# Linformer attention and an MLP mixer on one core: gated loads of batch 3, E and F cast by DMA, and the sums of two batches on one engine

## The chip, the core and the metric

The kernel runs on one core of one Trainium2 chip. The metric is the time in microseconds (us) that the device takes for one execution; lower is better. A second number, the span, is the time from the first to the last instruction of the one execution that was profiled; the profiled execution's own time is a little longer than its span.

## The reference

The inputs are q, k and v, each [8 batches, 8 heads, 1024 positions, 64], two projections E and F of shape [64, 1024], and four mixer weights, all float32. Cut to what is computed:

```python
k_proj = einsum('ks,bhsd->bhkd', E, k)             # 1024 positions -> 64
v_proj = einsum('ks,bhsd->bhkd', F, v)
scores = (q @ k_proj.T) / sqrt(64)
attn = exp(scores - max) / sum(exp(scores - max))
x = heads_side_by_side(attn @ v_proj)              # [8, 1024, 512]
h = relu(x.T @ w_tok1) @ w_tok2                    # mixes tokens, 1024 -> 256 -> 1024
u = x + h.T
out = u + relu(u @ w_ch1) @ w_ch2                  # mixes channels, 512 -> 1536 -> 512
```

## The kernel before

Batches are software-pipelined on one core. While TensorE works on the channel mixing of batch b (the "up" product with w_ch1, then the "down" product with w_ch2), the projections, attention and token mixing of the next batches are put between its steps. The order is written out by hand: every step of up and down has a cost in us (0.43, 0.66 and so on), the costs add up to a clock, and a list of items (time on that clock, function) says before which step an item is issued (lines 688 to 725). Each engine then executes its instructions strictly in the order in which they were issued.

**What a batch goes through.** load (line 85) reads q, k and v of a batch by DMA, issued on GpSimd (POOL), which also casts float32 to bfloat16; each of the three buffers exists once, so a load waits until the batch before has been read out of it. kv_step (line 228) projects k and v with E and F: 16 matmuls, in turn one that reads k and one that reads v (lines 157 and 162); after them it issues the three loads of the batch after. turn_q (line 99) transposes q by two DMAs on SyncE's queue (SP). score_step (189) and ou_step (202 to 214) are the attention of one head; the VectorE (DVE) instruction in line 209 writes x. tok1_steps (247) and tok2_steps (270) mix the tokens; line 273 adds x and so makes u. After every second slab of u a DMA transpose on SP (line 275) writes a quarter of uT, the left factor of the up product. SP holds these transposes, those of q and the output stores (line 599) in one order.

**Up and down.** Both are Strassen-Winograd products with seven partial products P1 to P7 (lines 518 and 576), apart from the up product of batch 0, which is plain (line 444). Winograd needs sums of quarter matrices: up_t (lines 496 to 502) makes T1, T2, T4 and a difference in place from uT; up_weights (472 to 478) makes those of w_ch1, down_weights (659) those of w_ch2, once each; up_sum (427 to 433) makes S1, S2, S4 and a difference in place from g, the activation between up and down. Up runs in three rounds of two slabs (i = 0, 2, 4); for every pair of slabs four sums fall due, one at each of the next four calls of up_sum. In line 425 `third` says who computes them: 0 POOL, 1 DVE for the first two and POOL for the last two, 2 DVE. In batch 0 a sum is 128x512 and there are six groups of four; from batch 1 on a sum is 128x1024 and there are three groups of four. relu_add (line 524) is DVE's step in up: it adds a saved partial product K to one in PSUM and clips at zero. In down, snap (line 482) saves a partial product on ScalarE (ACT) and POOL adds u to it (611, 625, 631).

**The front.** Before any of this the first batch is loaded in four pairs of heads. E and F come first, by two DMAs on SP in float32 into EF_f; ACT casts one half (line 146), DVE the other (147); TensorE transposes the result (150), and DVE copies it to EFT (151). Then come q's transposes on TensorE (315) and the first kv_step in pieces.

**The place that the change is named for.** kv_step(2) is issued at clock 34.4 of batch 0, and its loads of batch 3 were issued right behind it. At about the same clock tok2_steps(1) ends (30.0 to 34.2) and issues the last quarters of uT of batch 1. up_t(1) is issued at 37.1 and needs all four quarters; batch 1's up product cannot go past P2 before it. kv_step(3), the first user of batch 3's k and v, is issued 13.8 into batch 1.

Of the kernel before, what the change touches and what calls it, by code (L numbers as in the profile page):

```python
# [10 lines left out]
F32 = mybir.dt.float32  # L11
# [6 lines left out]
def kernel(  # L18
# [13 lines left out]
    nc = tc.nc  # L32
# [59 lines left out]
        )  # L92

    def load_all(b):
        load(b, "k", k)
        load(b, "v", v)
        load(b, "q", q)

    def turn_q(b):
        st["qT", b] = work.tile([P, H, 4, P], BF16, tag="qT", name="qT", bufs=1)  # L100
# [5 lines left out]
            )  # L106


    EF_f = work.tile([P, S], F32, tag="o1", name="EF_f", bufs=2)
    EF_sb = work.tile([P, S], BF16, tag="T1", name="EF_sb", bufs=1)  # L110
    nc.sync.dma_start(out=EF_f[0:KP], in_=E)
    nc.sync.dma_start(out=EF_f[KP:P], in_=F)
    wc1_v = moe_w_ch1.rearrange("(dc p) c -> p dc c", p=P)
    wc2_v = moe_w_ch2.rearrange("(cc p) d -> p cc d", p=P)

# [30 lines left out]
    nc.scalar.activation(out=EF_sb[:, 0:512], in_=EF_f[:, 0:512], func=ACT.Copy)  # L146
    nc.vector.tensor_copy(out=EF_sb[:, 512:S], in_=EF_f[:, 512:S])
    e_ps = b_ps("e_ps", BF16)
    for si in range(SC):
        nc.tensor.transpose(e_ps[:, si * P : (si + 1) * P], EF_sb[:, si::SC], ident)  # L150
    nc.vector.tensor_copy(out=EFT.rearrange("p s k -> p (s k)"), in_=e_ps)


    def k_mm(b, kv_ps, hs, si, f):
# [73 lines left out]
    def kv_step(b):  # L228
        st["kp", b] = work.tile([KP, H, 2, D], BF16, tag="kprojs", name="kprojs", bufs=1)
        st["kv", b] = kv_ps = front_ps("kv_ps")  # L230
        for si in range(SC):
            f = dict(start=(si == 0), stop=(si == SC - 1))
            k_mm(b, kv_ps, AL, si, f)
            v_mm(b, kv_ps, AL, si, f)
        k_out(b, kv_ps, AL)
        if b + 1 < B:
            load(b + 1, "q", q)
            load(b + 1, "k", k)
            load(b + 1, "v", v)

    def tok1_steps(b):
        def step(t, s0):
# [174 lines left out]
    def up_sum(b):  # L417

        if not st["sq", b]:
            return  # L420
        i, n, m = st["sq", b].pop(0)
        a11, a12, a21, a22 = (g_part(b, i, n, r, c) for c in range(2) for r in range(2))
        s1, s2, s4 = (x[:, i : i + n, :] for x in st["S", b])
        third = (i + n - 1) // 2
        eng = (nc.gpsimd, nc.gpsimd if m > 1 else nc.vector, nc.vector)[third]
        if m == 0:
            eng.tensor_add(out=s1, in0=a21, in1=a22)  # L427
        elif m == 1:
            eng.tensor_sub(out=s2, in0=s1, in1=a11)  # L429
        elif m == 2:  # L430
            eng.tensor_sub(out=a21, in0=a11, in1=a21)  # L431
        else:
            eng.tensor_sub(out=s4, in0=a12, in1=s2)  # L433
# [16 lines left out]
    def up_plain(b, part=()):  # L450

        g = st["g", b]
        for n in range(24):
            i, r = divmod(n, 4)
            cc, sh = (i, CH + i)[r // 2], r % 2
            up_mm(b, n, [DMC - 1] if n in part else range(DMC))
            o = g[:, cc, sh * 512 : (sh + 1) * 512]
            nc.scalar.activation(out=o, in_=st["g_ps", n], func=ACT.Relu)
            up_sum(b)
            if r == 3:  # L460
                up_sums(b, i, 1)
            if n in (6, 10, 14):
                up_weights((n - 6) // 4)
            yield 0.22 if n in part else 0.87
        up_weights(3)

    def up_weights(n):

# [94 lines left out]
    def down(b):  # L563
# [23 lines left out]
        def v2(t):  # L587
            return t.rearrange("p (e d) -> p e d", e=2)
# [12 lines left out]
        def part(j, m):  # L601
# [19 lines left out]
            elif m == 5:  # L621
                x["ga"] = c_ps("ga")
                yield from prod(x["ga"], "P5", j, True)
                x["K5"] = snap("K5", x["ga"])
                nc.gpsimd.tensor_add(out=v2(x["K5"]), in0=v2(x["K5"]), in1=u[:, bot, hi])  # L625
                if first:
                    down_weights(2)
            elif m == 6:
                yield from prod(x["be"], "P6", j)
                x["K2"] = snap("K2", x["be"])  # L630
                nc.gpsimd.tensor_add(out=v2(x["K2"]), in0=v2(x["K2"]), in1=u[:, top, hi])
                if first:
                    down_weights(3)
            elif m == 3:
                yield from prod(x["ga"], "P3", j, stop=True)
                nc.vector.tensor_add(out=x["o1"][:, :, hi], in0=v2(x["ga"]), in1=v2(x["K2"]))
                store(j, "o1", top)
            elif m == 7:
                yield from prod(x["be"], "P7", j)
                nc.vector.tensor_add(out=x["o2"][:, :, hi], in0=v2(x["be"]), in1=v2(x["K5"]))  # L640
                store(j, "o2", bot)
            else:
                yield from prod(x["be"], "P4", j, stop=True)
                nc.vector.tensor_add(out=x["o2"][:, :, lo], in0=v2(x["be"]), in1=u[:, bot, lo])
                store(j, "o2", bot)
# [43 lines left out]
    for b in range(B):  # L689
        up_us = 18.28 if b == 0 else 18.06  # L690
        dn = t0 + up_us
        if b == 0:
# [3 lines left out]
            add(t0 + 30.0, 0.6, tok2_steps(1))  # L696
            add(t0 + 37.1, 0.43, [lambda n=n: up_t(1, n) for n in range(4)])
            kv(t0 + 34.4, 2, 2.4)
            items.append((t0 + 29.6, lambda: turn_q(2)))
        else:  # L700
            if b == 1:
                attend(t0 + 1.0, 2, 1.3)
                add(t0 + 14.6, 0.45, tok1_steps(2))
                add(dn + 0.5, 0.8, tok2_steps(2))
# [51 lines left out]
```

## Time and profile before

| | us |
|---|---|
| median of 3 runs | 464.19 (463.48 to 465.42) |
| the profiled execution | 466.96 |
| its span | 465.2 |
| busy in the span: TensorE (PE) | 418.4 |
| VectorE (DVE) | 300.0 |
| GpSimd (POOL) | 224.4 |
| ScalarE (ACT) | 201.3 |

Times of instructions are counted from the start of the span. A row of the timeline gives the start, how long a run of like instructions took, the engine, the line in the kernel, out<-in, the shapes and how many there were; in square brackets stands how long the engine sat idle before it and what released it. A row of the windows gives, for one stretch, each engine's busy time and instruction count, then the clock granted to TensorE as a share of full speed, the DMA engines' busy share, and GB/s. A DMA row ends with the median time from issue to landing.

### The profile page before, as it was taken

To read this page: it belongs to the slowest core of one execution; us is meant where nothing else is said; L and a number is where in the kernel's file an instruction comes from. 1 tells how busy PE (TensorE), PEld (TensorE's weight loads), DVE (VectorE), ACT (ScalarE), POOL (GpSimd) and SP (SyncE) were. 2 spreads that over 40 slices of the span, in tenths; PEclk is the share of its full clock that TensorE was granted. 3 is DMA by queue.
4 is the path that set the end of the run, shared out by engine and by line. 5 is a ranking of instruction groups with operands and counts; after the bars stand their busy time and mean duration, and the time that the engine had idled before them with its cause. 6 is when DMAs were issued, how large, how long until landed. Compare 5 with 4: busy or idle time off the path is not lost.

```text
span 465.2 us, 7577 instructions
## 1 busy us (share of the span) xinstructions
PE 418.4 (90%) x2985; PEld 270.4 (58%) x3012; DVE 300.0 (64%) x500; ACT 201.3 (43%) x368; POOL 224.4 (48%) x161
## 2 busy tenths in 40 slices
PE   2779987991799999999999999999999999999896
PEld 2466445660344774478545874488447854685385
DVE  1545579360786767585867586767768686845842
ACT  2636662211465136533464345623762355316321
POOL 7431944230084262934394366637373439354841
PEclk9989998997699999999999999999999999999899
DMA  8999989699746968399529934994703420242013
GB/s 161 207 204 205 180 118 202 149 153 195 175 90 107 195 153 182 54 187 214 153 40 196 212 126 91 145 212 114 166 1 58 125 90 2 47 136 92 0 46 135
DMA packets 92691, 61.83 MB, mean 133 GB/s; under 512 B 59888, under 2 KB 88048, under 8 KB 92656
## 3 DMA queue, kind: packets, MB, share of 16 engines
q0 software_dynamic: 29200, 29.36, 39.5%
q1 hardware_dynamic: 63456, 31.99, 30.3%
q8 instruction: 23, 0.38, 0.3%
q14 instruction: 12, 0.10, 0.1%
HBM read 59.24 MB, written 16.78 MB: 163 GB/s over the span
## 4 chain that ended last, share of the span: by engine, by line
PE 72%; DVE 14%; DMA 7%; ACT 3%; issue 2%; SPq 0%; DVEq 0%; ACTq 0%
PE be L518 14%; PE be L576 14%; PE ga L518 7%; PE ga L576 6%; DMA uT<-u_sb 6%; PE h_ps L247 5%; PE al L576 4%; PE al L518 4%; PE g_ps L444 4%; PE u_ps L270 4%; DVE g L524 3%; PE ou_ps L202 3%; PE kv_ps L157 3%; DVE u_sb L273 2%; DVE x_sb L209 2%
## 5 line engine op out<-in xcount | busy, mean ns | idle before, releaser
L482 ACT ACTIVATE K<-be 128x512 f32<-128x512 f32 x116 | 67.1, 600 | 83.6 <-PE be L518 37.2
L576 PEld LDWEIGHTS <-g 128*128 128x128 bf16 x768 | 74.8, 98 | 17.5 <-issue 0.4
L576 PEld LDWEIGHTS <-S 128*128 128x128 bf16 x576 | 56.0, 98 | 12.0 <-issue 0.3
L194 ACT ACTIVATE attnT<-sco 128x512 bf16<-128x512 f32 x64 | 37.7, 595 | 53.0 <-PE sco L189 51.4
L427 POOL TENSOR_TENSOR S<-g 128x1024 bf16<-128x1024 bf16 (+1 forms) x9 | 17.2, 1907 | 85.3 <-DVE g L524 70.3
L611 POOL TENSOR_TENSOR K<-K,u_sb 128x512 f32<-128x512 f32 x16 | 19.2, 1198 | 69.2 <-ACT K L482 69.2
L518 PEld LDWEIGHTS <-wc 128*128 128x128 bf16 x336 | 32.1, 99 | 34.5 <-issue 1.5
L518 PEld LDWEIGHTS <-uS 128*128 128x128 bf16 x252 | 24.9, 100 | 44.7 <-issue 18.6
L576 PE MATMUL be<-wc,g 128*128 128x256 bf16 x384 | 49.3, 273 | 0.2
L273 DVE TENSOR_TENSOR u_sb<-u_ps,x_sb 128x512 bf16<-128x512 f32 x56 | 38.4, 687 | 12.3 <-PE u_ps L270 11.5
L518 PE MATMUL be<-uT,wc 128*128 128x512 bf16 x168 | 46.3, 385 | 0.0
L482 ACT ACTIVATE K<-ga 128x512 f32<-128x512 f32 x58 | 33.5, 608 | 29.3 <-PE ga L576 24.4
L209 DVE TENSOR_TENSOR x_sb<-ou_ps,rdn 128x512 bf16<-128x512 f32 x64 | 44.3, 692 | 2.2
L524 DVE CUSTOM_DVE_ANT_0 g<-be,K 128x512 bf16<-128x512 f32 x42 | 27.6, 686 | 23.4 <-PE be L518 22.7
L431 POOL TENSOR_TENSOR g<-g 128x1024 bf16<-128x1024 bf16 (+1 forms) x18 | 37.1, 2062 | 3.6 <-DVE S L427 3.6
L625 POOL TENSOR_TENSOR K<-K,u_sb 128x512 f32<-128x512 f32 x16 | 19.4, 1214 | 38.2 <-ACT K L482 38.2
L518 PE MATMUL be<-T,uS 128*128 128x512 bf16 x84 | 24.4, 391 | 13.2 <-DVE T L498 13.2
L433 POOL TENSOR_TENSOR S<-g,S 128x1024 bf16<-128x1024 bf16 (+1 forms) x18 | 35.4, 1967 | 0.7 <-DVE S L429 0.7
L202 PE MATMUL ou_ps<-vbd,attnT 128*128 128x130 bf16 x256 | 25.8, 225 | 10.8 <-DVE x_sb L209 8.3
L559 ACT ACTIVATE g<-be 128x512 bf16<-128x512 f32 x42 | 23.5, 596 | 25.3 <-PE be L518 25.3
L524 DVE CUSTOM_DVE_ANT_0 g<-al,K 128x512 bf16<-128x512 f32 x42 | 27.6, 686 | 7.5 <-PE al L518 4.4
L270 PE MATMUL u_ps<-R_sb,wt 128*128 128x512 bf16 x98 | 30.3, 379 | 2.3 <-DVE u_sb L273 1.9
(92 smaller groups left out, 766.9 us busy)
## 6 DMA issues: line engine op xcount, KB each, us to landing
out_dram<-o SPq DMA_DIRECT2D x32, 512.0 KB, 2.9
q_sb<-in_q_dram POOLq DMA_DIRECT2D x7, 1024.0 KB, 9.5
k_sb<-in_k_dram POOLq DMA_DIRECT2D x7, 1024.0 KB, 14.0
v_sb<-in_v_dram POOLq DMA_DIRECT2D x7, 1024.0 KB, 20.4
wc<-in_moe_w_ch_dram POOLq DMA_DIRECT2D x4, 384.0 KB, 14.8
wc<-in_moe_w_ch_dram POOLq DMA_DIRECT2D x2, 768.0 KB, 32.5
q_sb<-in_q_dram POOLq DMA_DIRECT2D x4, 256.0 KB, 7.7
k_sb<-in_k_dram POOLq DMA_DIRECT2D x4, 256.0 KB, 8.2
```

The costliest lines, as they stand in the source:

```text
L194: nc.scalar.activation(out=at, in_=sco, func=ACT.Exp, scale=scale)
L202: nc.tensor.matmul(ou[:, s // 2, o : o + 2 * D1], at[:, s * P : (s + 1) * P], vbd[:, h, :], start=True, stop=True,)
L209: nc.vector.tensor_tensor(out=st["x", b][:, :, h * D : (h + 1) * D].rearrange("p (b k) d -> p b k d", b=2), in0=ov[:, :, :, 0:D], in1=rdn[ ...
L270: nc.tensor.matmul(u_ps, wt2[:, t, s::SC], st["R", b][:, t, :], start=(t == 0), stop=(t == TC - 1))
L273: nc.vector.tensor_add(out=st["u", b][:, s, :], in0=u_ps, in1=st["x", b][:, s, :])
L431: eng.tensor_sub(out=a21, in0=a11, in1=a21)
L433: eng.tensor_sub(out=s4, in0=a12, in1=s2)
L482: nc.scalar.activation(out=t, in_=x, func=ACT.Copy)
L518: nc.tensor.matmul(acc, l[:, dc, i * P : (i + 1) * P], r[:, :, dc, :], start=start and dc == 0, stop=stop and dc == 1, skip_group_check=True,)
L524: nc.vector._custom_dve(TENSOR_ADD_SAT, out=o, in0=x, in1=y, s0=3.0e38, s1=0.0)
L559: nc.scalar.activation(out=g_part(b, i + e, 1, 1, 0)[:, 0], in_=be[e], func=ACT.Relu)
L576: nc.tensor.matmul(acc[:, e * HF : (e + 1) * HF], l[:, lc + c, l0 + (2 * j + e) * P : l0 + (2 * j + e + 1) * P], r[:, rc + c, r0 : r0 + HF ...
```

## The change

It has six edits. (1) kv_step(2) no longer issues the loads of batch 3. A new gated_load(3), an item at clock 1.5 of batch 1, first copies one column of uT of batch 1, from the slabs that the last quarter's transpose writes, on POOL, and then issues the three loads; they stand behind that copy in POOL's order. (2) E and F are loaded on POOL, cast by the DMA, ahead of the first loads of q, k and v; EF_f and its two casts go, and the copy to EFT is split between DVE and ACT. (3) `third` is 2 in the first and the last batch, so DVE makes all sums there. (4) up_weights(3) moves from the end of up of batch 0 to the end of part (j=1, P7) of down of batch 0, between DVE's eviction and the store. (5) turn_q(2) is issued at 25.2 instead of 29.6, which puts it ahead of one output store on SP. (6) load_all now issues q, k, v, the order that kv_step used.

```diff
+    nc.gpsimd.dma_start(out=EF_sb[0:KP], in_=E)
+    nc.gpsimd.dma_start(out=EF_sb[KP:P], in_=F)
-    nc.sync.dma_start(out=EF_f[0:KP], in_=E)
-    nc.sync.dma_start(out=EF_f[KP:P], in_=F)
...
-    nc.scalar.activation(out=EF_sb[:, 0:512], in_=EF_f[:, 0:512], func=ACT.Copy)
-    nc.vector.tensor_copy(out=EF_sb[:, 512:S], in_=EF_f[:, 512:S])
...
-    nc.vector.tensor_copy(out=EFT.rearrange("p s k -> p (s k)"), in_=e_ps)
+    nc.vector.tensor_copy(out=eft[:, 0:512], in_=e_ps[:, 0:512])
+    nc.scalar.activation(out=eft[:, 512:], in_=e_ps[:, 512:], func=ACT.Copy)
...
-        if b + 1 < B:
-            load(b + 1, "q", q)
-            load(b + 1, "k", k)
-            load(b + 1, "v", v)
+        if b + 1 < B and b != 2:
+            load_all(b + 1)
+
+    def gated_load(b, x):
+
+        gate = work.tile([P, 1], BF16, tag="gate", name="gate", bufs=1)
+        nc.gpsimd.tensor_copy(out=gate, in_=x)
+        load_all(b)
...
-        third = (i + n - 1) // 2
+        third = 2 if b in (0, B - 1) else (i + n - 1) // 2
...
-        up_weights(3)
...
                 nc.vector.tensor_add(out=x["o2"][:, :, hi], in0=v2(x["be"]), in1=v2(x["K5"]))
+                if (b, j) == (0, 1):
+                    up_weights(3)
                 store(j, "o2", bot)
...
-            items.append((t0 + 29.6, lambda: turn_q(2)))
+            items.append((t0 + 25.2, lambda: turn_q(2)))
...
+                items.append((t0 + 1.5, lambda: gated_load(3, st["uT", 1][:, SC - 1, DMC - 1, 0:1])))
```

Three places show what this does to the order of instructions. Lines of the changed kernel are two to four higher than those of before for the same code (up_sum is 430 to 436, relu_add 526, down_weights 663, the POOL adds 613 to 633).

POOL where batch 0 goes over into batch 1. K_... are the saved partial products of down of batch 0, S_... and g belong to up of batch 1. Before:

```order
L625 TENSOR_TENSOR K_1053<-K_1053,u_sb 128x512
L631 TENSOR_TENSOR K_1082<-K_1082,u_sb 128x512
L90 DMA q_sb<-in_q_dram 128x8x512
L90 DMA k_sb<-in_k_dram 128x8x512
L90 DMA v_sb<-in_v_dram 128x8x512
L427 TENSOR_TENSOR S_1194<-g 128x1024
```

The changed kernel in the same place:

```order
L627 TENSOR_TENSOR K_1053<-K_1053,u_sb 128x512
L633 TENSOR_TENSOR K_1079<-K_1079,u_sb 128x512
L241 COPY gate<-uT 128x1
L90 DMA q_sb<-in_q_dram 128x8x512
L90 DMA k_sb<-in_k_dram 128x8x512
L90 DMA v_sb<-in_v_dram 128x8x512
L430 TENSOR_TENSOR S_1186<-g 128x1024
```

The loads keep their place among POOL's instructions, but the gate now stands ahead of them, and behind it stand the sums of batch 1.

DVE where up of batch 0 goes over into down of batch 0. x_sb<-ou_ps is the attention of batch 1, wc_68 is w_ch1, dT_72 the first difference of w_ch2. Before:

```order
L433 TENSOR_TENSOR S_136<-g,S_135 128x512
L208 RECIPROCAL rdn<-ou_ps 128x8
L209 TENSOR_TENSOR x_sb<-ou_ps,rdn 128x8x64
L478 TENSOR_TENSOR wc_68<-wc_68 128x2x768
L427 TENSOR_TENSOR S_134<-g 128x512
L659 TENSOR_TENSOR dT_72<-wc_69 128x1536
L208 RECIPROCAL rdn<-ou_ps 128x8
L209 TENSOR_TENSOR x_sb<-ou_ps,rdn 128x8x64
```

The changed kernel:

```order
L436 TENSOR_TENSOR S_134<-g,S_133 128x512
L207 RECIPROCAL rdn<-ou_ps 128x8
L208 TENSOR_TENSOR x_sb<-ou_ps,rdn 128x8x64
L430 TENSOR_TENSOR S_132<-g 128x512
L663 TENSOR_TENSOR dT_72<-wc_69 128x1536
L207 RECIPROCAL rdn<-ou_ps 128x8
L208 TENSOR_TENSOR x_sb<-ou_ps,rdn 128x8x64
```

up_weights(3), the row with wc_68, has left this place; it now stands between the second and the last pair of u_sb of batch 1.

DVE in up of batch 7, rounds i = 2 and the start of i = 4. g<-al, g<-be and g<-ga are relu_add. Before:

```order
L524 ISA g<-ga,K_4719 128x512
L524 ISA g<-al,K_4752 128x512
L524 ISA g<-al,K_4758 128x512
L524 ISA g<-be,K_4782 128x512
L524 ISA g<-be,K_4787 128x512
L524 ISA g<-ga,K_4773 128x512
L524 ISA g<-ga,K_4777 128x512
L427 TENSOR_TENSOR S_4692<-g 128x1024
L429 TENSOR_TENSOR S_4693<-S_4692,g 128x1024
```

The changed kernel:

```order
L526 ISA g<-ga,K_4719 128x512
L430 TENSOR_TENSOR S_4692<-g 128x1024
L432 TENSOR_TENSOR S_4693<-S_4692,g 128x1024
L526 ISA g<-al,K_4752 128x512
L434 TENSOR_TENSOR g<-g 128x2x512
L526 ISA g<-al,K_4758 128x512
L436 TENSOR_TENSOR S_4694<-g,S_4693 128x1024
L526 ISA g<-be,K_4782 128x512
L526 ISA g<-be,K_4787 128x512
```

Four sums that POOL made beside DVE now stand in DVE's own order, two ahead of the two relu_adds of P2 and two between and behind them; the next round gets two more than it had.

More of the change, by code (lines that the diff above doesn't have):

```diff
@@ L94, in load_all @@
     def load_all(b):
+        load(b, "q", q)
         load(b, "k", k)
         load(b, "v", v)
-        load(b, "q", q)
     def turn_q(b):
@@ L106, in turn_q @@
             )
-    EF_f = work.tile([P, S], F32, tag="o1", name="EF_f", bufs=2)
     EF_sb = work.tile([P, S], BF16, tag="T1", name="EF_sb", bufs=1)
-    nc.sync.dma_start(out=EF_f[0:KP], in_=E)
-    nc.sync.dma_start(out=EF_f[KP:P], in_=F)
+    nc.gpsimd.dma_start(out=EF_sb[0:KP], in_=E)
+    nc.gpsimd.dma_start(out=EF_sb[KP:P], in_=F)
     wc1_v = moe_w_ch1.rearrange("(dc p) c -> p dc c", p=P)
@@ L150 @@
         nc.tensor.transpose(e_ps[:, si * P : (si + 1) * P], EF_sb[:, si::SC], ident)
-    nc.vector.tensor_copy(out=EFT.rearrange("p s k -> p (s k)"), in_=e_ps)
+    eft = EFT.rearrange("p s k -> p (s k)")
+    nc.vector.tensor_copy(out=eft[:, 0:512], in_=e_ps[:, 0:512])
+    nc.scalar.activation(out=eft[:, 512:], in_=e_ps[:, 512:], func=ACT.Copy)
     def k_mm(b, kv_ps, hs, si, f):
```

## The prediction

> **What bounds the kernel now.** I read the page first, then the table of waits, then windows around each place where TensorE (PE) stands still. The page gives PE nearly the whole span:
>
> ```profile
> PE 418.4 (90%) x2985; PEld 270.4 (58%) x3012; DVE 300.0 (64%) x500; ACT 201.3 (43%) x368; POOL 224.4 (48%) x161
> ```
>
> So a gain can only be PE's idle time, or time at a lower clock. The waits name the largest: PE's P6 of batch 1 waits for DVE, and DVE for a transpose.
>
> ```profile
> DVE T L496 <- DMA uT<-u_sb: 14.7, 2, 12.6
> ...
> PE be L518 <- DVE T L498: 13.2, 1, 13.2
> ```
>
> The windows show three stalls (PE's busy time is the second number), and behind each one a stretch at clock 0.50; the row from 119.30 to 138.70 covers batch 1's up as far as kv_step(3).
>
> ```profile
> 68.10:72.20 4.10, 0.03 (x1) 0.00 (x0) 4.07 (x6) 0.05 (x1) 4.10 (x3) 0.99 1.14 178
> 72.20:75.50 3.30, 3.28 (x17) 2.32 (x18) 2.59 (x5) 0.60 (x1) 0.13 (x1) 0.50 1.22 201
> 105.80:119.30 13.50, 0.33 (x3) 0.05 (x2) 1.41 (x3) 0.53 (x1) 0.00 (x0) 0.64 1.21 218
> 119.30:123.30 4.00, 4.00 (x13) 1.71 (x13) 2.82 (x6) 2.28 (x4) 0.00 (x0) 0.50 1.20 251
> 119.30:138.70 19.40, 18.39 (x99) 8.39 (x98) 16.68 (x32) 12.54 (x23) 9.94 (x5) 0.90 0.53 103
> ...
> 437.30:440.70 3.40, 3.40 (x10) 1.17 (x8) 1.18 (x3) 1.19 (x2) 3.04 (x2) 0.50 0.00 0
> ```
>
> In the chain of waits the last quarter of uT of batch 1 takes 17.80 us from issue to its user, those of batches 2 and 3 take 4.77 and 3.89:
>
> ```profile
> 99.90 17.80 DMA uT<-u_sb
> ...
> 164.17 4.77 DMA uT<-u_sb
> ...
> 214.47 3.89 DMA uT<-u_sb
> ```
>
> What differs is what runs beside it. The timeline has the three loads of batch 3 issued from 98.12 on, and the DMA engines are full until 119.30 (share 1.21):
>
> ```profile
> 98.12 0.92 POOL L90 DMA_DIRECT2D q_sb<-in_q_dram  x1 [3.82 <-DMA qT<-q_sb]
> ...
> 101.26 0.87 POOL L90 DMA_DIRECT2D k_sb<-in_k_dram  x1 [2.21 <-PE kv_ps L162]
> ...
> 102.35 0.89 POOL L90 DMA_DIRECT2D v_sb<-in_v_dram  x1 [0.22 <-issue]
> ...
> 117.83 0.69 DVE L496 TENSOR_TENSOR T<-uT 128x1024 bf16<-128x1024 bf16 x1 [12.57 <-DMA uT<-u_sb]
> ...
> 119.30 1.87 PE L518 MATMUL be<-T,uS 128*128 128x512 bf16 x4 [13.17 <-DVE T L498]
> ...
> 138.69 0.40 PE L157 MATMUL kv_ps<-k_sb,EFT 128*64 128x512 bf16 x1
> ```
>
> **The gate.** Without the loads the last quarter should need 4.3 us, between 3.89 and 4.77. It starts later, though: up_weights(3) now stands on DVE ahead of the last two evictions of u, and costs what a 128x1536 difference costs alone, 0.95 us (row below), some of it in a gap; I charge 0.8. uT is there at 99.9 + 0.8 + 4.3 = 105.0. P6 follows 119.30 - 117.83 = 1.5 later, at 106.6, 12.7 us earlier than before. Without that idle time the 4.00 us at clock 0.50 go as well: 2.0 us. So PE would be ready for kv_step(3) at 138.69 - 14.7 = 124.0. DVE had 16.68 us of work in these 19.40 us and hardly lets PE come sooner.
>
> What is late next is batch 3's v: kv_step(3) reads k and v in turn. Behind the gate POOL issues q at about 105.3 (the copy of one column is bounded by nothing and by 0.9, a DMA issue), k at 106.2 and v at 107.1. Behind those stand only POOL's sums of batch 1, not due until well after. v's landing time after issue was 22.4 us in the loads of batch 3, 18.3 in those of batch 2 and 19.9 in those of batch 4:
>
> ```profile
> v_sb<-in_v_dram POOLq DMA_DIRECT2D x1, 1024.0 KB, 22.4
> ...
> v_sb<-in_v_dram POOLq DMA_DIRECT2D x1, 1024.0 KB, 18.3
> ...
> v_sb<-in_v_dram POOLq DMA_DIRECT2D x1, 1024.0 KB, 19.9
> ```
>
> I take 19, since the transposes that slowed the first are done and those of q of batch 3 come only near the end. v is there at 126.1, 2.1 us after PE is ready: the gain is 138.69 - 126.1 = **12.6 us**. The ends: landing after 22.4, with one more stretch at clock 0.50 (3.40 us, half of it lost: 1.7), leaves 138.69 - 129.5 - 1.7 = 7.5; PE held by nothing but DVE gives 14.3.
>
> By the Trainium skill ("TensorE: Matmul & The Clock Gate", Part 1: The HAM clock gate) the half rate comes after at least one idle window of about 3.4 us; by that a wait of 2.1 us would cost no clock. This trace differs: the 2.06 us wait at 436.93 (below) was followed by 3.40 us at 0.50. By the row the sum would be 1.7 us smaller, by the page as it stands.
>
> turn_q(2) moves past one store on SP: q's transposes go out earlier, in part beside batch 2's loads, and only the first score of batch 2, well into batch 1, needs them. I cost this at nothing; if the cover were gone, the gate would wait for the SP queue and the term above would shrink towards its lower end.
>
> **Sums of batch 0 on DVE.** Beside POOL's sums DVE's own took up to 1.37 us, alone 0.42. Twelve more at 0.42 are 5.0 us, spread over up of batch 0, where PE waits for nothing on DVE. What counts is the turn from up to down:
>
> ```profile
> 55.30 1.37 DVE L427 TENSOR_TENSOR S<-g 128x512 bf16<-128x512 bf16 x1
> ...
> 62.58 0.42 DVE L431 TENSOR_TENSOR g<-g 128x512 bf16<-128x512 bf16 x1
> ...
> 66.28 1.93 DVE L478 TENSOR_TENSOR wc<-wc 128x1536 bf16<-128x1536 bf16 x1
> ...
> 69.42 1.90 DVE L659 TENSOR_TENSOR dT<-wc 128x1536 bf16<-128x1536 bf16 x1
> ...
> 71.24 0.20 DVE L208 RECIPROCAL rdn<-ou_ps 128x8 f32<-128x8 f32 x1
> ...
> 72.22 0.61 PE L202 MATMUL ou_ps<-vbd,attnT 128*128 128x130 bf16 x4 [4.09 <-DVE x_sb L209]
> ...
> 74.83 0.95 DVE L659 TENSOR_TENSOR dT<-wc,dT 128x1536 bf16<-128x1536 bf16 x1
> ```
>
> Three DVE steps delay the reciprocal at 71.24. L478 leaves; the sum and L659 remain. At the prices alone they end at 66.3 + 0.4 + 0.95 = 67.7, a gain of 3.5; at the slowed ones at 66.3 + 1.4 + 1.9 = 69.6, a gain of 1.6. No sum runs on POOL any more, so I take the first, **3.4 us**. The 3.30 us at clock 0.50 give little beyond, as DVE is the limit behind them; half of what they cost goes into the upper end, 4.1.
>
> **Sums of batch 7 on DVE.**
>
> ```profile
> 425.84 1.08 ACT L559 ACTIVATE g<-be 128x512 bf16<-128x512 f32 x2 [1.39 <-PE be L518]
> 426.07 1.03 PE L518 MATMUL be<-uT,wc 128*128 128x512 bf16 x4
> ...
> 428.66 1.03 PE L518 MATMUL ga<-T,uS 128*128 128x512 bf16 x4
> ...
> 432.12 1.03 PE L518 MATMUL be<-uT,wc 128*128 128x512 bf16 x4
> ...
> 433.78 2.50 DVE L429 TENSOR_TENSOR S<-S,g 128x1024 bf16<-128x1024 bf16 x1
> ...
> 436.93 1.61 PE L518 MATMUL ga<-T,uS 128*128 128x512 bf16 x4 [2.06 <-DVE g L524]
> ...
> 442.11 1.47 PE L576 MATMUL be<-wc,g 128*128 128x256 bf16 x12
> ...
> 443.06 0.69 DVE L429 TENSOR_TENSOR S<-S,g 128x1024 bf16<-128x1024 bf16 x1
> ```
>
> Round i = 2 takes 432.12 - 426.07 = 6.05 us, round i = 4 takes 9.99: a sum slowed to 2.50 holds up P2's relu_adds, P5 finds no free bank for 2.06 us, and the clock falls. That loss of 3.9 goes, but now three sums stand ahead of the second relu_add of P2 in both rounds. They start when ACT has written g, 0.85 into the round, and that relu_add ends 0.85 + 3 x 0.69 + 2 x 0.65 = 4.2 in (0.65 from the pairs' spacing, an estimate); P5's second half wants the bank at 428.66 + 0.43 - 426.07 = 3.0. PE waits 1.2 in each round, 2.5 in all. The gain is 3.9 - 2.5 = **1.4 us**; ends -0.5 (a clock drop again) and 3.8.
>
> **E and F.**
>
> ```profile
> 4.07 0.72 POOL L90 DMA_DIRECT2D q_sb<-in_q_dram  x1
> ...
> 8.87 0.43 PE L150 MATMUL e_ps<-ident,EF_sb 128*128 128x128 bf16 x2 [8.87 <-ACT EF_sb L146]
> ...
> 12.69 0.61 PE L315 MATMUL qt_ps<-ident,q_sb 128*128 128x128 bf16 x4
> ```
>
> PE starts at 8.87 behind the cast. It can start up to 2 us sooner, but needs the second pair of heads next, which PE used at 12.69 and which landed near 11 (6.8 us after 4.07):
>
> ```profile
> q_sb<-in_q_dram POOLq DMA_DIRECT2D x1, 256.0 KB, 6.8
> ```
>
> Two more issues at 0.72 stand ahead of every load. So the gain lies between -0.5 and 1.2; I take **0.5 us**.
>
> **Sum.** 12.6 + 3.4 + 1.4 + 0.5 = 17.9 us. The profiled execution took 466.96 (span 465.2), so 449.1; it stands 2.8 above the median of the runs, 464.19, and carried over to that the forecast is **446.3 us**. The ends of all terms are 8.1 and 23.4, or 440.8 to 456.1.
>
> **Rivals.** *The wait moves to kv_step(3).* The loads now start late, beside two output stores, and q's transposes of batch 3 cross the last of them. If v lands 24 us after issue, at 131, and the clock drops (1.7), the gate's term is 6.0 and the time 452.9. For it: 22.4 with transposes beside. Against: those were four quarters in the middle of the loads. Chance 0.20.
>
> *The change does not free uT.* If the transposes were slow for another reason than the loads, or the gate let the loads go too early, 12.6 would vanish: 458.9. The 4.77 and 3.89 speak against it. Chance 0.07.
>
> *DVE becomes the bound in batches 0 and 7: slower.* If the moved sums kept their slowed prices, twelve at 1.37 and six at 2.50 are 31.4 us of DVE. If half of that lies on the path (an estimate; the page has DVE busy for 64%), 15.7 us are lost and the 3.4 and 1.4 with them, against 13.1 kept: 2.6 us slower, 466.8. It decides where more than 13.1 of the 31.4 us lie on the path. For it: DVE fills the stall at 68.10 (4.07 of 4.10). Against: the prices alone, 0.42 and 0.69, make 9.2 us, less than the 13.1 if all of it lay there, and POOL has no sums in these batches. Chance 0.07.
>
> **How the numbers follow.** The forecast has 0.66. 441.5 to 455 holds nearly all of it and the first rival; outside lie the other two and the tails, about 0.2. A measurement of this kernel can tell about 0.5%, 2.3 us, from no change: faster 0.92 (forecast, first rival, most of the second), same 0.03, slower 0.05.
>
> **What would show it.** The wait of T (L496 before) for uT under 1 us; no clock of 0.50 between the start of batch 1 and kv_step(3); PE's kv_step(3) idle 1 to 4 us on v_sb; the reciprocal wait at the start of down of batch 0 about 1 us; two waits near 1.2 us in batch 7 and no sum on DVE above 1 us there. I am wrong if uT still takes over 8 us, if PE stands at kv_step(3) for over 6, or if DVE's sums stay above 1 us.

## The result and the profile after

| | before | changed |
|---|---|---|
| median of 4 runs, us | 464.81 (463.48 to 465.75) | 453.01 (452.44 to 454.44) |
| the profiled execution, us | 466.96 | 452.44 |
| its span, us | 465.2 | 450.7 |

The ratio is 0.9753, 95% interval 0.9716 to 0.9789. Of the runs below, one execution of before (2442.84 us) and one of turn_late (462.22 us, at a granted clock of 0.938 on average) lie far outside the others and are left out. The time lies in the range of the forecast and 6.7 us above its value: by the profiled executions 14.5 us were gained where the sum said 17.9, by the medians 11.8. The page of the changed kernel gives PE a larger share of a shorter span; POOL lost 28 us of work. DVE took it over and is 1.2 us below before all the same: beside POOL's sums a 128x512 sum had taken it up to 1.37 us and a 128x1536 difference 1.9, and now they take about 0.42 and 0.95; the cast of half of E and F and half of the copy to EFT, 0.7 us together, are gone too.

```profile
PE 417.6 (93%) x2985; PEld 270.4 (60%) x3012; DVE 298.8 (66%) x517; ACT 201.1 (45%) x368; POOL 196.3 (44%) x146
```

In the table of waits of the changed kernel (total, times, longest) P6's wait of 13.2 us for DVE's T has shrunk to 0.6. DVE's wait of 12.6 us for uT is gone; a wait for uT of 9.3 us stands on POOL's gate instead, where PE does not feel it. Behind the first instruction's wait at the start of the kernel, PE's longest are now x_sb in the turn from up to down of batch 0 and v in kv_step(3).

```profile
POOL gate L241 <- DMA uT<-u_sb: 9.3, 1, 9.3
...
PE ou_ps L201 <- DVE x_sb L208: 7.0, 7, 3.4
...
PE kv_ps L161 <- DMA v_sb<-in_v_dram: 2.4, 2, 2.1
...
PE be L520 <- DVE T L500: 0.6, 1, 0.6
```

The windows show the same. Before, PE was busy for 14.87 of the 29 us from 96 to 125:

```profile
96.00:125.00 29.00, 14.87 (x92) 8.00 (x93) 11.66 (x20) 7.05 (x12) 2.68 (x3) 0.76 1.10 187
```

In the changed kernel it is busy for 24.15 of them, at clock 1.00. The stall of batch 0's turn is still there (first row), and behind it and behind the wait for v there is a stretch at half clock. The last two rows belong to a point that comes below: the share of the DMA engines is 1.07 in the first 160 us and 0.53 in the rest.

```profile
69.00:72.44 3.44, 0.00 (x1) 0.01 (x1) 3.41 (x6) 0.60 (x1) 1.54 (x1) 1.00 1.20 192
...
73.50:76.90 3.40, 2.97 (x17) 2.07 (x16) 2.69 (x5) 1.19 (x2) 0.15 (x1) 0.51 1.24 208
96.00:125.00 29.00, 24.15 (x153) 11.91 (x154) 24.39 (x43) 16.40 (x30) 15.15 (x10) 1.00 1.02 177
124.50:128.00 3.50, 3.50 (x16) 1.52 (x16) 0.00 (x0) 0.18 (x1) 0.87 (x1) 0.54 0.96 206
0.00:160.00 160.00, 135.59 (x1043) 87.54 (x1052) 96.60 (x182) 71.68 (x131) 56.89 (x61) 0.98 1.07 180
160.00:450.70 290.70, 281.97 (x1944) 182.85 (x1961) 202.25 (x335) 129.46 (x237) 139.42 (x86) 1.00 0.53 113
```

The timeline of the changed kernel answers the rows that were shown of before:

```profile
64.84 0.88 POOL L90 DMA_DIRECT2D q_sb<-in_q_dram  x1 [34.79 <-DMA qT<-q_sb]
65.71 0.88 POOL L90 DMA_DIRECT2D k_sb<-in_k_dram  x1
66.58 0.89 POOL L90 DMA_DIRECT2D v_sb<-in_v_dram  x1
67.47 1.19 POOL L613 TENSOR_TENSOR K<-K,u_sb 128x512 f32<-128x512 f32 x1
68.69 0.69 DVE L619 TENSOR_TENSOR o<-al,K 128x512 f32<-128x512 f32 x1 [1.34 <-POOL K L613]
...
70.16 1.38 DVE L434 TENSOR_TENSOR g<-g 128x512 bf16<-128x512 bf16 x1
...
72.44 0.40 PE L201 MATMUL ou_ps<-vbd,attnT 128*128 128x130 bf16 x4 [3.44 <-DVE x_sb L208]
...
94.96 0.95 DVE L480 TENSOR_TENSOR wc<-wc 128x1536 bf16<-128x1536 bf16 x1
...
96.56 0.38 PE L156 MATMUL kv_ps<-k_sb,EFT 128*64 128x512 bf16 x1 [0.95 <-DVE u_sb L276]
...
100.29 0.19 POOL L241 COPY gate<-uT 128x1 bf16<-128x1 bf16 x1 [9.26 <-DMA uT<-u_sb]
...
102.58 0.91 POOL L90 DMA_DIRECT2D v_sb<-in_v_dram  x1
...
104.24 1.02 PE L520 MATMUL be<-T,uS 128*128 128x512 bf16 x4 [0.62 <-DVE T L500]
...
124.47 0.38 PE L161 MATMUL kv_ps<-v_sb,EFT 128*64 128x512 bf16 x1 [2.12 <-DMA v_sb<-in_v_dram]
...
417.47 0.59 PE L520 MATMUL ga<-T,uS 128*128 128x512 bf16 x2 [0.61 <-DVE g L526]
...
424.43 0.59 PE L520 MATMUL ga<-T,uS 128*128 128x512 bf16 x2 [0.61 <-DVE g L526]
```

Read it in two places. At the turn of batch 0, POOL is free of sums, but its first add to K stands behind the three loads of batch 2, which wait until q of batch 1 has been transposed: they go out at 64.84 (before at 65.10, row below), although PE is 2.5 us ahead by then (64.37 against 66.87 for the same instruction). DVE's step at 68.69 waits for that add, and PE's step at 72.44 for DVE. This is the row of before:

```profile
65.10 0.91 POOL L90 DMA_DIRECT2D q_sb<-in_q_dram  x1 [7.42 <-DMA qT<-q_sb]
```

At the gate, all is as the prediction had it: the copy, the three issues, PE at P6 15.06 us earlier (119.30 - 104.24), and then v, 21.85 us after its issue by the chain of waits:

```profile
102.58 21.85 DMA v_sb<-in_v_dram
```

PE executes the same instructions in the same order in both kernels, so the start of one instruction can be compared across traces. This table has the start of four of them, and the span, for the profiled execution of each kernel that leaves PE's order as it is at these places: PE's ou step of batch 0's turn (72.44 above), P6 of batch 1 (104.24 above), the ou step of batch 3's attention in down of batch 1 (158.72), and a step at 300 us. The names are those of the experiments below.

| kernel | turn of batch 0 | P6 of batch 1 | attention of batch 3 | at 300 us | span |
|---|---|---|---|---|---|
| before | 77.02 | 119.30 | 171.38 | 312.93 | 465.2 |
| changed | 72.44 | 104.24 | 158.72 | 300.05 | 450.7 |
| changed, again | 73.27 | 104.76 | 159.37 | 300.71 | 451.3 |
| gate_alone | 76.62 | 106.36 | 158.83 | 300.26 | 450.9 |
| no_gate | 72.59 | 116.33 | 168.82 | 310.16 | 460.8 |
| kv_first | 72.39 | 103.06 | 162.45 | 306.07 | 456.8 |
| ef_old | 72.66 | 105.14 | 160.23 | 301.57 | 451.7 |
| b0_pool_sums | 75.76 | 108.40 | 162.98 | 304.54 | 454.8 |
| b7_pool_sums | 73.06 | 104.07 | 157.71 | 299.05 | 451.9 |
| kv_late | 72.52 | 103.14 | 156.91 | 298.25 | 448.6 |
| load2_late | 72.38 | 104.35 | 160.69 | 302.03 | 452.7 |
| best | 70.71 | 101.86 | 157.02 | 298.52 | 448.8 |
| best_ef | 70.37 | 101.80 | 157.18 | 300.19 | 450.5 |

The lead over before is 4.6 us at the turn of batch 0, 15.1 at P6 and 12.7 at 158.72; nothing changes then until batch 7, and the last 150 us add 1.6 more (12.9 at 300 us, 14.5 in the span).

### The profile page after: what moved, and what is told of

Same layout as the page of the kernel before. It is cut to its first block, busy times and chain, and to the rows that moved or that the text cites. A ratio compares the mean times of both kernels' runs of the same rounds, so it can differ in the third digit from the quotient of the medians.

```text
span 450.7 us, 7576 instructions
## 1 busy us (share of the span) xinstructions
PE 417.6 (93%) x2985; PEld 270.4 (60%) x3012; DVE 298.8 (66%) x517; ACT 201.1 (45%) x368; POOL 196.3 (44%) x146
## 4 chain that ended last, share of the span: by engine, by line
PE 71%; DVE 14%; DMA 8%; issue 2%; ACT 2%; POOL 1%; DVEq 0%; POOLq 0%; ACTq 0%
PE be L578 14%; PE be L520 12%; PE ga L578 7%; PE ga L520 6%; PE h_ps L250 5%; DMA v_sb<-in_v_dram 5%; PE al L578 4%; PE g_ps L447 4%; PE u_ps L273 4%; PE al L520 3%; DVE g L526 3%; PE kv_ps L156 3%; PE ou_ps L201 3%; DVE u_sb L276 2%; DMA uT<-u_sb 2%
## 5 line engine op out<-in xcount | busy, mean ns | idle before, releaser
L526 DVE CUSTOM_DVE_ANT_0 g<-be,K 128x512 bf16<-128x512 f32 x42 | 27.4, 685 | 20.9 <-PE be L520 20.4
L430 POOL TENSOR_TENSOR S<-g 128x1024 bf16<-128x1024 bf16 x6 | 12.7, 2124 | 47.9 <-DVE g L526 47.9
L250 PE MATMUL h_ps<-x_sb,wt 128*128 128x512 bf16 x102 | 31.0, 379 | 0.7 <-ACT R_sb L255 0.3
L201 PEld LDWEIGHTS <-attnT 128*128 128x128 bf16 x256 | 18.3, 99 | 20.2 <-DVE x_sb L208 10.6
L434 POOL TENSOR_TENSOR g<-g 128x1024 bf16<-128x1024 bf16 x12 | 26.6, 2216 | 3.6 <-DVE S L430 3.6
```

Of the source, the lines that this page charges most:

```text
L201: nc.tensor.matmul(ou[:, s // 2, o : o + 2 * D1], at[:, s * P : (s + 1) * P], vbd[:, h, :], start=True, stop=True,)
L250: nc.tensor.matmul(st["h", b][:, t, :], wt1[:, s, t * P : (t + 1) * P], st["x", b][:, s, :], start=(s == 0), stop=(s == SC - 1),)
L526: nc.vector._custom_dve(TENSOR_ADD_SAT, out=o, in0=x, in1=y, s0=3.0e38, s1=0.0)
```

## The experiments

Theory A, formed on these traces: the gate alone makes the gain, and what the other edits win before about 125 us is waited out where PE next needs a transfer. Its main rival, B, is named at each run. Each kernel was timed in turn with before; the medians of before were 466.1 us beside the first four kernels and 465.77 beside the other eight.

**gate_alone.** Before, with the gate and the order of load_all only:

```diff
-        if b + 1 < B:
-            load(b + 1, "q", q)
...
+        if b + 1 < B and b != 2:
+            load_all(b + 1)
...
+                items.append((t0 + 1.5, lambda: gated_load(3, st["uT", 1][:, SC - 1, DMC - 1, 0:1])))
```

> The kernel before, with the gated loads of batch 3 and nothing else of the change. Theory A (the loads beside them made the transposes of uT slow, so the gate alone frees them): P6 of batch 1 starts about 13 us earlier, some 2 to 4 us of that go again where kv_step(3) waits for v and the clock halves, and the time is 9 to 12 us below before, 453 to 456. Theory B (uT is late because the transposes of q of batch 2 stand right ahead of its own on SP, so it is the earlier turn_q(2) that frees it): uT still comes late and the time is less than 5 us below before.

Measured: 453.19 us, ratio 0.9748 (0.9704 to 0.9792). That is the time of the whole change, and P6 starts 12.9 us earlier than in before, as A said. The two traces are level at 158.8, although gate_alone comes to P6 2.1 us later. Its timeline has a shorter wait for v, and no half clock behind it (the window's clock is 1.00):

```profile
125.90 0.38 PE L162 MATMUL kv_ps<-v_sb,EFT 128*64 128x512 bf16 x1 [1.42 <-DMA v_sb<-in_v_dram]
```

```profile
126.00:130.00 4.00, 4.00 (x26) 1.94 (x26) 1.11 (x2) 1.90 (x4) 1.68 (x2) 1.00 0.84 179
```

**no_gate.** The changed kernel with kv_step(2) issuing the loads of batch 3 again; the other five edits stay:

```diff
-        if b + 1 < B and b != 2:
+        if b + 1 < B:
...
-                items.append((t0 + 1.5, lambda: gated_load(3, st["uT", 1][:, SC - 1, DMC - 1, 0:1])))
```

> The changed kernel with the loads of batch 3 back behind kv_step(2), everything else of the change kept. Theory A: the last quarter of uT takes over 12 us again, P6 of batch 1 waits 10 us or more, and the time is 8 to 12 us above the changed kernel, 461 to 465. Theory B: the earlier turn_q(2) alone keeps uT early, and the time stays within 2 us of the changed kernel's 453.

Measured: 464.39 us, ratio 0.9955 (0.9928 to 0.9981). In the waits the old stall is back, as A said, so neither q's earlier transposes nor the moved up_weights(3) freed uT. By its trace the five edits bring 4.4 us (465.2 - 460.8), by the medians 1.7.

```profile
PE be L520 <- DVE T L500: 12.3, 1, 12.3
```

**kv_first.** The gated loads in the order k, v, q, so that v lands sooner:

```diff
         nc.gpsimd.tensor_copy(out=gate, in_=x)
-        load_all(b)
+        load(b, "k", k)
+        load(b, "v", v)
+        load(b, "q", q)
```

> The changed kernel with the gated loads in the order k, v, q. Theory A (the 2.1 us wait of kv_step(3) for v, and the 3.4 us at clock 0.50 behind it, are a real cost of the gate): v lands about 17 us after the gate instead of 24, the wait is gone, the clock stays at 1.00, and the time is 2.5 to 4 us below the changed kernel, 449 to 450.5. Theory B (the wait only moves): q lands last, turn_q(3) and with it the loads of batch 4 come later, a wait of the same size appears in batch 2, and the time stays at 453.

Measured: 457.53 us, ratio 0.9836 (0.9794 to 0.9877): slower than the changed kernel by about 4 us. The wait for v is gone, and PE is 5 us ahead of the changed kernel behind it (122.62 against 127.72 for the same instruction of batch 1's up). But q now lands last, its transposes end late, the loads of batch 4 wait for them (8.13 us, first row) and meet the transposes of uT of batch 2: the collision that the gate removed from batch 1 is back one batch later, and half clock beside it (the window's clock is 0.50). So B had the way, and the price is higher than it said.

```profile
132.32 0.92 POOL L90 DMA_DIRECT2D q_sb<-in_q_dram  x1 [8.13 <-DMA qT<-q_sb]
...
160.13 0.69 DVE L500 TENSOR_TENSOR T<-uT 128x1024 bf16<-128x1024 bf16 x1 [9.01 <-DMA uT<-u_sb]
162.45 0.61 PE L201 MATMUL ou_ps<-vbd,attnT 128*128 128x130 bf16 x4 [7.71 <-DVE x_sb L208]
```

```profile
156.70:166.90 10.20, 4.45 (x22) 3.13 (x23) 4.88 (x9) 0.60 (x1) 4.65 (x2) 0.50 0.42 135
```

**turn_late.** q's transposes of batch 2 back behind the output store:

```diff
-            items.append((t0 + 25.2, lambda: turn_q(2)))
+            items.append((t0 + 29.6, lambda: turn_q(2)))
```

> The changed kernel with turn_q(2) back at clock 29.6. Theory A: the transposes of q of batch 2 are quick without loads beside them and SP reaches those of uT in time; within 1 us of the changed kernel, 452 to 454. Theory B: uT is late by the 4 to 6 us that q's transposes take, and the time is 457 or more.

Measured: 453.23 us, ratio 0.9747 (0.971 to 0.9785): no difference, as A said.

**ef_old.** E and F loaded and cast as before:

```diff
-    nc.gpsimd.dma_start(out=EF_sb[0:KP], in_=E)
-    nc.gpsimd.dma_start(out=EF_sb[KP:P], in_=F)
+    nc.sync.dma_start(out=EF_f[0:KP], in_=E)
+    nc.sync.dma_start(out=EF_f[KP:P], in_=F)
...
+    nc.scalar.activation(out=EF_sb[:, 0:512], in_=EF_f[:, 0:512], func=ACT.Copy)
+    nc.vector.tensor_copy(out=EF_sb[:, 512:S], in_=EF_f[:, 512:S])
...
+    nc.vector.tensor_copy(out=EFT.rearrange("p s k -> p (s k)"), in_=e_ps)
```

> The changed kernel with E and F loaded in float32 on SP and cast by ACT and DVE, as before; all else as changed. Theory A: the front gives about 1 us by its own work (e_ps starts 3.6 us later, of which 1.1 us is left at q's first turn) and up to 1 us more where the half-clock window of 27.7 to 31.1 us falls away; so 0.5 to 2.5 us slower than the changed kernel, 454 to 455.5 us. Rival B: what the front gains is waited out at the loads of batch 2, and the time stays at 453 us.

Measured: 452.2 us, ratio 0.9707 (0.9672 to 0.9742): not slower at all, so B holds here and A's 0.5 to 2.5 us does not. PE begins 4.1 us later (9.37), is 1.1 us late at 22 us and, behind a half-clock stretch from 23.45 to 26.86 that the first trace of the changed kernel does not have, 1.7 late at 28 us. At the turn of batch 0 it is 0.2 late, as it waits that much less there (1.37 against 3.44 us):

```profile
72.66 0.40 PE L202 MATMUL ou_ps<-vbd,attnT 128*128 128x130 bf16 x4 [1.37 <-DVE x_sb L209]
```

**b0_pool_sums and b7_pool_sums.** The sums of one batch given to POOL and DVE as before:

```diff
-        third = 2 if b in (0, B - 1) else (i + n - 1) // 2
+        third = 2 if b == B - 1 else (i + n - 1) // 2
```

> The changed kernel with the sums of batch 0 given to POOL and DVE as before; the sums of batch 7 stay on DVE. Theory A: the gain was eaten by the new 3.4 us wait for x_sb at 72.4 us, as POOL's add to K stands behind the loads of batch 2, which wait for q's transposes of batch 1; so what is given back is the net of about 1 us, 453 to 455 us. Rival B: the prediction's term of 3.4 us is right and the loss is elsewhere: about 456.5 us.

Measured: 454.58 us, ratio 0.9741 (0.9698 to 0.9785). In the trace the turn of batch 0 is 3.3 us later with a wait of 4.48; 1.7 of these belong to the loads of batch 2, which left at 66.54 here and at 64.84 in the changed kernel. The rest is near A's net of 1 us, as are the medians, 1.4 us over the changed kernel's 453.14 (below), but the intervals of the ratios overlap. This profiled execution was the slowest of its six (456.64; the fastest 451.44).

```profile
75.76 0.61 PE L201 MATMUL ou_ps<-vbd,attnT 128*128 128x130 bf16 x4 [4.48 <-DVE x_sb L208]
```

```diff
-        third = 2 if b in (0, B - 1) else (i + n - 1) // 2
+        third = 2 if b == 0 else (i + n - 1) // 2
```

> The changed kernel with the sums of batch 7 given to POOL and DVE as before; the sums of batch 0 stay on DVE. Theory A: the wait of 2.06 us in P5 of batch 7's down comes back instead of 0.61 us, with or without a half-clock window of 3.4 us behind it: 1 to 4 us slower, 454 to 457 us. Rival B: the tail's wait is hidden elsewhere, 453 us.

Measured: 454.96 us, ratio 0.9762 (0.9724 to 0.98). In the trace the old slow sum (2.50 us beside POOL) and the old wait are back, with half clock behind it, and the stretch from 300 us to the end takes 152.9 us instead of 150.7. That is A; the medians agree (1.8 us), though the intervals of the ratios overlap.

```profile
420.25 2.50 DVE L432 TENSOR_TENSOR S<-S,g 128x1024 bf16<-128x1024 bf16 x1
...
423.40 1.36 PE L520 MATMUL ga<-T,uS 128*128 128x512 bf16 x4 [2.07 <-DVE g L526]
```

```profile
424.50:428.00 3.50, 3.50 (x10) 1.27 (x9) 2.02 (x3) 0.79 (x2) 2.32 (x2) 0.54 0.00 0
```

**kv_late.** kv_step(3) is issued later, behind 22 more matmuls and their weight loads, which need no transfer:

```diff
-                kv(t0 + (13.8 if b == 1 else 9.5), b + 2, 3.0)
+                kv(t0 + (16.4 if b == 1 else 9.5), b + 2, 3.0)
```

> The changed kernel with kv_step(3) issued at 16.4 of batch 1 instead of 13.8, so that TensorE has about 45 other instructions to do while v lands. Theory A: the 2.1 us wait for v and the half-clock window behind it go, the loads of batch 4 start late by no more than 2 us and find no other transposes: 2 to 3.5 us faster than the changed kernel, 449.5 to 451 us. Rival B: later loads of batch 4 meet the transposes of uT of batch 2, as they did where the gated loads came k, v, q, and the wait only moves there: 453 us or more.

Measured: 451.81 us, ratio 0.9696 (0.966 to 0.9732). kv_step(3) no longer waits for v, and no half clock follows. Behind the part whose order differs PE is 2.2 us ahead of the changed kernel (141 to 157 us), and 1.8 us at the attention of batch 3. So A was right about the wait, and B about the rest, if not quite by its way. The loads of batch 4 are hardly later (127.26 to 130.30 against 128.30 to 130.06), but PE now comes sooner to uT of batch 2 behind them: DVE's T waits 2.50 us for it (1.50 in the changed kernel).

```profile
154.59 0.69 DVE L498 TENSOR_TENSOR T<-uT 128x1024 bf16<-128x1024 bf16 x1 [2.50 <-DMA uT<-u_sb]
...
156.91 0.40 PE L201 MATMUL ou_ps<-vbd,attnT 128*128 128x130 bf16 x4 [1.20 <-DVE x_sb L208]
```

**after_again.** The changed kernel unchanged, as a yardstick for the last runs.

> The changed kernel once more, unchanged, beside the three that follow: 453 us, a ratio of 0.975 to before. If it lies at 451.5 us or less, the gaps of under half a per cent that other runs showed against it mean nothing.

Measured: 453.14 us, ratio 0.9735 (0.9706 to 0.9764); with the first four runs the median of nine is 453.14 too. The wait for v is longer here than in the first trace, and yet no half clock follows it (the window's clock is 1.00).

```profile
125.87 0.38 PE L161 MATMUL kv_ps<-v_sb,EFT 128*64 128x512 bf16 x1 [3.00 <-DMA v_sb<-in_v_dram]
```

```profile
125.90:129.40 3.50, 3.50 (x23) 1.72 (x23) 0.68 (x1) 1.33 (x3) 0.00 (x0) 1.00 0.92 198
```

**load2_late.** The loads of batch 2 right behind POOL's first add to K instead of right ahead of it:

```diff
-        if b + 1 < B and b != 2:
+        if b + 1 < B and b not in (1, 2):
...
+            items.append((t0 + 21.5, lambda: load_all(2)))
```

> The changed kernel with the loads of batch 2 issued on POOL right behind the first add to K of batch 0's down instead of right ahead of it. Theory A: the K that this add takes is saved by 65.2 us, but POOL issues the three loads until 67.5 us first; with the add ahead, DVE's sum at 68.69 us and with it the wait of 3.44 us for x_sb at 72.4 us shrink by 1.5 to 2.3 us, and the loads start 1.2 to 1.5 us later, with 10 us to spare before kv_step(2): 450.5 to 452 us. Rival B: DVE, which now makes all sums of batch 0, is the wait's cause and not POOL's place: the time stays at 453 us.

Measured: 454.17 us, ratio 0.9747 (0.972 to 0.9774): nothing gained, so A's number fails. The wait at the turn is 1.24 us instead of 3.44, but that alone does not show POOL's place to be its cause: PE came to the turn 2.2 us later than in the first trace of the changed kernel (66.52 against 64.37, behind a half-clock stretch from 27.40 to 30.81), and no_gate, whose loads still stand ahead of the add, waits 1.37 us when it comes that late (66.38). best, below, shows it: it comes at 64.85, waits 1.24 and is through the turn at 70.71. So A's cause holds and B's does not. What A had wrong is that it put the later loads at nothing, and followed on SP they are not. They leave 3.7 us later, v of batch 2 lands at 93.3 instead of 86.6, q's two transposes beside them run for 14.84 us on SP's queue instead of 9.64, the transposes of uT of batch 1 behind them start at 94.84 instead of 89.95, the gate opens at 102.84 instead of 100.29, and PE waits 4.0 us for v instead of 2.1.

```profile
72.38 0.40 PE L201 MATMUL ou_ps<-vbd,attnT 128*128 128x130 bf16 x4 [1.24 <-DVE x_sb L208]
...
79.27 14.84 SPq L103 DMA_TRANSPOSE qT<-q_sb  x2
...
94.84 5.99 SPq L278 DMA_TRANSPOSE uT<-u_sb  x4
...
102.84 0.19 POOL L241 COPY gate<-uT 128x1 bf16<-128x1 bf16 x1 [12.52 <-DMA uT<-u_sb]
```

The row of q's transposes in the changed kernel, and in gate_alone, where the loads of batch 2 had landed before (84.7):

```profile
79.57 9.64 SPq L103 DMA_TRANSPOSE qT<-q_sb  x2
```

```profile
89.39 5.91 SPq L103 DMA_TRANSPOSE qT<-q_sb  x2
```

**best and best_ef.** kv_late and load2_late together, with up_weights(3) after P7 of j=0 (DVE is idle there); and the same with E and F as in ef_old:

```diff
-                if (b, j) == (0, 1):
+                if (b, j) == (0, 0):
                     up_weights(3)
```

> The changed kernel with kv_step(3) at 16.4, the loads of batch 2 behind the first add to K, and up_weights(3) in the first half of down of batch 0 (after P7 of j=0). Theory A: three waits of their own, 2 to 3 us, 1.5 to 2.3 us and 0.9 us, that add up: 447.5 to 449.5 us. Rival B: the transfers that all wait for each other set the pace, and the best of the three alone is all there is: 451 us.

> The same three edits with E and F loaded in float32 on SP and cast by ACT and DVE, as before the change. Theory A (the front's gain is waited out at the loads of batch 2, and E and F are worth nothing): the same as with the three edits alone, within 1 us. Rival B: now that the wait for x_sb is smaller, the 1 to 2 us of the front come through, and it is slower by that.

Measured: best 454.58 us (448.75 to 455.39), ratio 0.974 (0.9694 to 0.9786); best_ef 453.18, ratio 0.9726 (0.97 to 0.9752). The gains do not add up: best has 1.8 us more than kv_late at the turn of batch 0 and 1.3 at P6, and is level with it at the attention of batch 3 (157.02 and 156.91), where PE waits 2.60 us instead of 1.20. That is the rival of the expectation; its 451 is near the profiled execution (450.61), and the median lies above it (last section). best_ef stays within 0.8 us of best from 12.3 to 158 us and then loses 1.8 in a half-clock stretch (158.39 to 161.80): E and F are worth nothing here either.

```profile
70.71 0.40 PE L201 MATMUL ou_ps<-vbd,attnT 128*128 128x130 bf16 x4 [1.24 <-DVE x_sb L208]
...
157.02 0.40 PE L201 MATMUL ou_ps<-vbd,attnT 128*128 128x130 bf16 x4 [2.60 <-DVE x_sb L208]
```

No version beats the changed kernel clearly. kv_late comes nearest: its median is 1.3 us lower, its trace 2.1 us shorter, and the intervals of the two ratios overlap.

## Why the prediction was right in kind and too large

**The gate: right, in mechanism and size.** 12.6 us were forecast. The kernel with the gate alone gains 12.9 by the medians and 12.6 by the traces at the attention of batch 3 (171.38 - 158.83). The steps in the changed kernel: P6 ran 15.06 us earlier, of which 3.3 were there at 79 us already, so 11.8 where 12.7 were forecast; uT was free at 100.29, but DVE had other steps to do ahead of T, and PE waited 0.62 us for it. The charge for up_weights(3), 0.8, was a wait of 0.95 at kv_step(2). The half clock of 4.0 us went and gave 1.7 where 2.0 were forecast (from P6 to kv_step(3) PE takes 119.30 to 138.69 in before and 104.24 to 121.95 here). The wait for v was forecast at 2.1 and was 2.12; that is partly luck, since v took 21.85 us instead of 19 and was issued sooner, and the wait was 1.42 in gate_alone and 3.00 in the changed kernel's second trace. The half clock behind it, which the prediction kept for the term's lower end, came in one execution of the changed kernel and not in the other.

**What failed: the sum.** The step "12.6 + 3.4 + 1.4 + 0.5 = 17.9" added terms that share waits, at two places.

The front and the sums of batch 0 share the wait for x_sb. PE came to the turn at 64.37, 2.5 us ahead of before and 2.9 ahead of gate_alone (1.0 and 1.4 by the front's own work, the rest because both of those had a half-clock stretch at 28 to 31 us and this trace had none). But in the kernels that make the sums of batch 0 on DVE and keep the loads ahead of POOL's first add, the turn starts between 72.39 and 73.27, whether PE comes to it at 64.37 (changed) or at 66.38 (no_gate): who comes early waits longer.

The batch 0 terms and the gate share the landing of v: PE goes on when v is there. I worked out that landing on the clock of before, and then let the 3.9 us of batch 0 and the front move it by as much. They did not. Set beside gate_alone, which lacks them, the changed kernel leads by 4.2 us at the start of the turn, by 2.7 at its end, by 2.1 at P6 (up_weights(3) cost 0.8 on the way), by 2.4 at the gate (100.29 against 102.71) and by 1.4 when v has landed (124.47 against 125.90), as v takes 21.85 us and not 20.50. The half clock behind the wait then takes these 1.4: both kernels are at the next step of up at 127.72. In the changed kernel's second trace no half clock follows, but v takes 22.74 us and the lead is gone when it lands (125.87).

The transfers form a chain of their own. The loads of batch 2 leave at 64.7 to 65.1 us in before, in gate_alone and in the changed kernel's first trace, and by 66.5 in all kernels that keep their place; they wait for q's transposes of batch 1, not for PE. From them hang q's transposes of batch 2, on SP behind those uT of batch 1, the gate, the loads of batch 3, q's transposes of batch 3, the loads of batch 4, and beside these uT of batch 2. Not every link is tight: in the changed kernel the last quarter of uT goes out at 97.14, when DVE has written its u, so the gate there still follows the engines, while in load2_late and kv_late the four transposes follow each other on SP without a gap. kv_first, kv_late, load2_late and best each took a wait out at one link and found it again, in part or more, at a later one. The DMA engines' share of 1.07 over the first 160 us fits that: there is no room in which a transfer that starts late could catch up. That it is the cause is argued from the shares; no run here had fewer bytes to move.

**Sums of batch 0: near the forecast size at the turn, and worth nothing at the end.** 3.4 us were forecast, 3.9 with the front; at the turn's end (79.02 and 82.30 for the same instruction) the lead is 3.3. The sign "the reciprocal wait about 1 us" failed: PE waits 3.44 us for x_sb, since the prediction looked at POOL's sums and not at the loads that stand ahead of POOL's first add, for which DVE waits 1.34. One DVE sum took 1.38 us beside POOL's add, the other 23 took 0.41 to 0.43.

**Sums of batch 7: right in size, with the clock's help.** 1.4 us were forecast; from the attention of batch 3 to the end before needs 293.8 us (465.2 - 171.38), the changed kernel 292.0, so 1.8. P5 waits twice 0.61 and not 1.2. In gate_alone, where the wait of 2.06 us is still there but no half clock follows, the same stretch takes 292.1: without the clock drop the edit is worth 0.1. b7_pool_sums, with the drop, loses 2.2. So the gain was the clock's, and whether the clock drops behind such a wait is a matter of where it falls (last section).

**E and F: 0.5 forecast, nothing found.** PE starts 3.6 us earlier, where the prediction gave 2 at most, and waits for q's second pair, as it said; 1.1 us are left there, and the turn of batch 0 takes them.

**The rivals.** The first gave 452.9 and 453.0 was measured, but not by its way: v did not take 24 us, and the gate's term was not 6.0. The second falls with gate_alone. The third falls with the sums of batch 7, all at 0.68 or 0.69 us, and those of batch 0, all but one at 0.43 or less.

What stays open is a remainder of some 2 us: the five other edits bring 4.4 us in one trace of no_gate and 1.7 in its medians, and single edits of the changed kernel shift its median by less than its executions differ among themselves.

## What to carry to other kernels

Before gains are added up, mark where the path goes through a transfer: what is won ahead of it counts only if the transfer's own chain (buffer free, load, transpose, next load) starts earlier by as much. Read the DMA engines' share in that stretch first; here it was full, and taking out one wait moved most of it to a later transfer. Two gains ahead of one wait do not add up either: the larger one counts. A gate that keeps a load from a transpose that PE waits for was worth nearly the whole stall here (12.6 of 13.2 us), because the load had almost enough time behind it.

## What the runs showed of the hardware

Which wait costs clock is not a matter of its length alone. In each of these traces the clock changes only at points that lie whole multiples of 3.41 us apart: in the changed kernel it is 0.50 from 73.57 to 76.98 and from 124.77 to 128.18, and 124.77 - 73.57 = 51.20 = 15 x 3.413. Cut each trace into pieces at these points. From 32 to 446 us, all pieces at clock 1.00 in which PE was busy for 1.40 us or less were followed by half clock, and none in which it was busy for 1.57 us or more. The wait of 2.12 us for v in the changed kernel lies whole in one piece (first row); that of 3.00 us in its second trace is cut in two by a point (the other rows).

```profile
121.36:124.77 3.41, 1.29 (x9) 0.42 (x8) 2.95 (x3) 0.60 (x2) 2.72 (x2) 1.00 1.29 172
```

```profile
121.30:124.71 3.41, 1.57 (x7) 0.50 (x6) 3.41 (x4) 1.18 (x2) 2.72 (x2) 1.00 1.30 153
124.71:128.12 3.41, 2.25 (x17) 1.16 (x17) 0.12 (x1) 0.32 (x1) 1.18 (x1) 1.00 1.27 208
```

In the same way half clock followed waits of 2.06 us (before, PE busy for 1.36 of the piece), 2.07 (b7_pool_sums, 1.33) and 2.84 (best_ef, 1.21), and didn't follow waits of 2.06 (gate_alone, 1.91) and 2.60 (best, 1.94). All waits of 3.3 us and more behind the start had half clock in them or behind them (3.31 in gate_alone, 3.44 here, up to 13.17 before). Where the points lie differs from trace to trace (72.08 in before, 74.75 in b0_pool_sums). The Trainium skill ("TensorE: Matmul & The Clock Gate", Part 1: The HAM clock gate) asks for at least one idle window of about 3.4 us; the pieces of 3.41 us agree with that length, but those with up to 1.40 us of work in them, which were followed by half clock, disagree with "idle". Most profiled executions also have a stretch at half clock between 20 and 32 us with no long wait ahead of it, behind pieces in which PE was busy for up to 1.93 us, so that busy time is not the whole rule. Kernels that are the same up to 60 us have that stretch (kv_first, kv_late, b7_pool_sums) or don't (changed, best).

That sets how far one execution can be trusted. best took 448.75 us at a mean clock of 0.998, 450.61 at 1.000, and 454.49 to 455.39 at 0.983 to 0.986: one program, over 6 us. Traces show where time goes, but a gain of 2 us in one pair of traces was no gain in the medians.

DMA transposes slow down beside loads, and loads beside transposes: q's two of batch 2 took 7.8 us each (median) from issue to landing in the changed kernel and 11.7 in load2_late, where they began only 10.8 us after the loads (79.27 - 68.50) instead of 14.7 (79.57 - 64.84); in gate_alone, where they began 24.7 us after them and the loads had landed, they took 5.3. v of batch 2 took 18.2 us in gate_alone, 20.0 in the changed kernel and 23.1 in load2_late. In the kernels with the gate that load q first, v of batch 3 took 20.4 to 22.7 us.
